# Attention and gated unit for one decoded token: the programs of ScalarE and VectorE aligned to a block of 256 instructions

## The chip, the cores and the metric

The kernel runs on one core of a Trainium2 chip. The metric is the device time of one execution, in microseconds, as the median of several runs; lower is better. The core has five engines with a program each: TensorE (PE), VectorE (DVE), ScalarE (ACT), GpSimd (POOL) and SyncE (SP), and 16 DMA engines that all of them share.

## The reference

One token `x` (512 values) is normalized and goes two ways: through attention with 32 heads over a cache of 8192 keys and values per head (128 wide), and through a gated unit of width 1376. The result is combined with `x`. All data are float32.

```python
x = A_x                                                        # 1 x 1 x 512
xn = _layernorm(x)
q = (xn @ A_wq).reshape(1, 1, 32, 128)                         # by heads
scores = einsum("bhqd,bhkd->bhqk", q, A_k_cache) * 128 ** -0.5 # 32 x 8192
o = einsum("bhqk,bhkd->bhqd", softmax(scores), A_v_cache)
s = o.reshape(1, 1, 4096) @ A_wo
h = sigmoid(xn @ B_w_gate) * (xn @ B_w_up)
g = silu(h @ B_w_down)
out = x + s * g
```

The two caches are 134 MB each, `A_wq` and `A_wo` 8.4 MB each.

## The kernel before, in words

The program is written out engine by engine, with semaphores set and waited for by hand inside one critical section; no scheduler moves anything. Helpers record each operation: `Steps` counts an engine's finished operations in its semaphore, `wait` makes an engine wait for such counts, and `load` (L131) issues a transfer.

The 32 heads are taken in 16 pairs. One pair's keys are one load of 8 MB into a buffer of 128 partitions by 64 KB, and so are its values. There are three such buffers: `slots[0]` and `slots[1]` take the keys of even and odd pairs, `slots[2]` takes `wq` at first, then the values of one pair after the other, and at the end the weights of the gated unit. SyncE issues all large loads on its queue: `wq`, the keys of pairs 0 and 1, then by turns values and keys, then the gated unit's weights, then `wo` in six pieces.

The start: ScalarE issues the load of `x_col` (2 KB) as its first work and `x_row` as its second (both through L131); VectorE fills constants (L168 to L176). When `x_col` is there, VectorE, TensorE and ScalarE normalize it (L180 to L198). TensorE multiplies with `wq` (L206), ScalarE copies the rows (L211), TensorE spreads each row over the partitions (L218), and ScalarE copies these into `q_all` (L225), two copies per 512 columns, which serve two pairs. Values of pair 0 are issued by SyncE (L161) when TensorE is done with `wq`.

The loop over pairs i:

- VectorE (`scores`): the product of keys and query in place (L281), its sum over each head's 128 columns (L282), and the maximum of the sums per partition (L284). It waits for the keys of pair i and the copies of the query. When L282 of pair i - 2 is done, SyncE may load the keys of pair i into the same buffer.
- TensorE (`pair`): turns the maxima (L246), spreads them (L248), sums the powers (L250), multiplies the powers with the values (L255), and picks the heads out of the result (L260). The first 15 pairs are a loop in TensorE's program, the last is written out.
- ScalarE (`powers_of`, `parts`, `place`): the scale of the maximum (L294), the exponentials (L296), the copy of the product with the values (L301), and the loads that put finished heads in their place in `o_all`.
- VectorE (`all_max`, `heads_out`): the maximum over a pair (L276), the quotient (L288, L289).
- When TensorE has done L255 of pair i, SyncE may load the next values.

Only TensorE's program has a loop; those of the other engines are written out in full. TensorE's loop is opened by this line, whose `head_slot` puts the loop's first instruction at the beginning of a block of 256 instructions:

```python
with nc.Fori(0, NP - 1, engines=OrderedEngineSet([PE.engine]), head_slot={PE.engine: 0}):
```

It does that with the directive that the change uses: an `addr_align` of 256 instructions, offset 0, `max_nops=0`. In the order of instructions it is an entry "ISA" on TensorE ahead of the loop's branch.

The end: TensorE computes the gated unit (L356 to L392, with VectorE and ScalarE), then the product with `wo` as its pieces land (L402, L406), and VectorE combines (L416, L418); SyncE issues the store.

The critical section is entered by all engines after SyncE's signal (L67); ahead of it ScalarE has one instruction that adds 16 to the semaphore `s_out`, which SyncE waits for at the end.

Of the kernel before, what the change touches and what calls it, by code (L numbers as in the profile page):

```python
# [18 lines left out]
def kernel(  # L19
# [40 lines left out]
    PE, DVE, ACT, SP, POOL = nc.tensor, nc.vector, nc.scalar, nc.sync, nc.gpsimd  # L60

    s_out = tc.alloc_semaphore("s_out")
    ACT.nop().then_inc(s_out, 16)
    section = ctx.enter_context(ExitStack())
# [391 lines left out]
```

## Time and profile before

| | before |
|---|---|
| median of 3 runs | 687.58 us |
| lowest and highest | 687.45 and 687.75 us |
| profiled execution: span from first to last instruction | 685.6 us |
| busy: VectorE | 574.0 us (84%) |
| busy: TensorE | 222.1 us (32%) |
| busy: ScalarE | 40.9 us (6%) |
| read from memory | 293.74 MB, 428 GB/s over the span |

The three runs were made without the profiler. Of the profiled execution the profile gives the span, not a time of its own beyond it; the 2.0 us between span and median lie around the first and last instruction.

How to read the rows that follow: a row of the order of time has the start and the length in us, the engine ("SPq" and "ACTq" are the issues of transfers by SyncE and ScalarE), the line, the operation, and in brackets the idle time before it and who ended it. A row of a DMA queue has the queue, the kind of its packets, their number, the megabytes, and the time that they took as a share of 16 engines. The kind "hardware_dynamic" is a kernel's transfers (q1 those that SyncE issues, q10 ScalarE's); the kind "instruction" is the loading of an engine's program. A row of a transfer's issue ends with the KB where they are given and the us from issue to landing. A row of stretches has the stretch, its length, the busy time of TensorE, its weight loads, VectorE, ScalarE and GpSimd, the clock granted to TensorE, the DMA share and the GB/s.

### The profile page before, as it was taken

The numbers are of one execution on the slowest core, as the hardware profiler recorded it, in microseconds if no ns is written. First come the engines' busy times: TensorE is split into PE (matmuls) and PEld (weight loads), VectorE is DVE, ScalarE is ACT, GpSimd is POOL, SyncE is SP. The second block draws the span as 40 slices with busy tenths as digits, with TensorE's granted clock in tenths as the row PEclk, the third lists the DMA queues.
The fourth block names the chain that finished last, engine by engine and source line by source line (L and its number), as shares of the span: only waits on it lengthen the run. The fifth ranks groups of instructions, "written<-read, shape, count | busy, mean of one in ns | idle before, by whom it ended". The sixth has DMA issues, their size and how long they took to land.

```text
span 685.6 us, 3694 instructions
## 1 busy us (share of the span) xinstructions
PE 222.1 (32%) x1570; PEld 62.7 (9%) x1570; DVE 574.0 (84%) x136; ACT 40.9 (6%) x122; POOL 0.7 (0%) x6
## 2 busy tenths in 40 slices
PE   0550230605041140505042140506042140605656
PEld 0110000101010010101001010101000010101121
DVE  0159999999999999989898989989898989989220
ACT  0040100000000000000001010000001010000010
POOL 0000000000000000000000000000000000000000
PEclk9965575757566575757557575756657575756798
DMA  9999999999999999999999999999999999999996
GB/s 375 440 445 451 428 428 428 432 428 428 428 436 444 448 440 428 428 428 436 428 428 428 440 444 451 428 432 428 432 432 428 428 440 436 451 436 428 405 434 285
DMA packets 6614, 293.84 MB, mean 429 GB/s; under 512 B 1096, under 2 KB 1104, under 8 KB 1616
## 3 DMA queue, kind: packets, MB, share of 16 engines
q1 hardware_dynamic: 6200, 293.74, 99.1%
q10 hardware_dynamic: 408, 0.02, 0.0%
q8 instruction: 4, 0.07, 0.0%
q14 instruction: 2, 0.02, 0.0%
HBM read 293.74 MB, written 0.00 MB: 428 GB/s over the span
## 4 chain that ended last, share of the span: by engine, by line
DMA 37%; DVE 30%; PE 0%; SPq 0%; issue 0%
DMA slot<-in_A_k_cache_dram 31%; DVE slot L281 15%; DVE sc L282 15%; DMA slot<-in_A_wo_dram 6%; PE acc L406 0%; SPq L131 0%; PE pt L246 0%; PE acc L377 0%; DVE g_row L416 0%; DVE g_row L418 0%; DVE mx L276 0%
## 5 line engine op out<-in xcount | busy, mean ns | idle before, releaser
L281 DVE TENSOR_TENSOR slot<-slot,q_all 128x16384 f32<-128x16384 f32 x16 | 275.5, 17217 | 38.8 <-DMA slot<-in_A_k_cache_dram 38.8
L282 DVE TENSOR_REDUCE sc<-slot 128x128 f32<-128x16384 f32 x16 | 275.5, 17220 | 0.6
L255 PE MATMUL po<-slot,weights 128*8 128x512 f32 x1024 | 146.7, 737 | 232.1 <-PEq L242 231.5
L255 PEld LDWEIGHTS po<-slot,weights 128*8 128x8 f32 x1024 | 30.3, 103 | 335.3 <-issue 334.6
L246 PE MATMUL pt<-ident,mx 128*1 128x128 f32 x32 | 8.8, 374 | 148.6 <-PEq L242 148.6
L301 ACT COPY o<-po 128x512 f32<-128x512 f32 x16 | 9.4, 586 | 385.2 <-PE po L255 385.2
L260 PE MATMUL pn<-o,pick 128*2 128x128 f32 x128 | 16.5, 272 | 12.8 <-PEq L242 12.8
L180 DVE TENSOR_REDUCE st<-x_col 128x1 f32<-128x4 f32 x1 | 0.2, 157 | 20.7 <-DMA x_col<-in_A_x_dram 20.7
L246 PEld LDWEIGHTS pt<-ident,mx 128*1 128x1 f32 x32 | 1.8, 80 | 154.1 <-issue 154.1
L288 DVE RECIPROCAL rl<-pn 2x1 f32<-2x1 f32 x16 | 2.3, 146 | 14.6 <-PE pn L260 14.6
L294 ACT ACTIVATE nb<-pm 128x2 f32<-128x2 f32 x16 | 2.8, 173 | 190.4 <-PE pm L248 190.4
L416 DVE TENSOR_TENSOR g_row<-g_row,acc 128x128 f32<-128x128 f32 x1 | 0.3, 289 | 15.3 <-PE acc L406 15.3
L296 ACT ACTIVATE weights<-sc,nb 64x128 f32<-64x128 f32 x32 | 12.8, 399 | 0.9
L260 PEld LDWEIGHTS pn<-o,pick 128*2 128x2 f32 x128 | 9.9, 84 | 29.6 <-issue 27.2
L248 PE MATMUL pm<-mx,ones 1*128 1x2 f32 x32 | 8.8, 344 | 7.4 <-PEq L242 7.4
L402 PE MATMUL big<-slot,o_all 128*1 128x512 f32 x56 | 9.4, 765 | 4.8 <-DMA slot<-in_A_wo_dram 4.8
L250 PE MATMUL pn<-rs,half 128*2 128x1 f32 x32 | 3.0, 163 | 23.5 <-PEq L242 23.5
L218 PE MATMUL big<-q_all,ones 1*128 1x512 f32 x16 | 8.8, 850 | 1.6 <-ACT q_all L225 0.8
L206 PE MATMUL big<-slot,xn 128*1 128x512 f32 x64 | 9.0, 726 | 0.8 <-DVE xn L198 0.8
L248 PEld LDWEIGHTS pm<-mx,ones 1*128 1x128 f32 x32 | 7.9, 306 | 14.4 <-issue 14.4
L276 DVE TENSOR_REDUCE mx<-pt 1x2 f32<-1x128 f32 x16 | 4.5, 278 | 5.2 <-PE pt L246 5.0
L182 PE MATMUL pt<-st,ones 128*128 128x1 f32 x2 | 0.6, 362 | 23.4 <-DVE st L180 23.4
(61 smaller groups left out, 62.1 us busy)
## 6 DMA issues: line engine op xcount, KB each, us to landing
slot<-in_A_wo_dram SPq DMA_DIRECT2D x1, 3584.0 KB, 32.5
slot<-in_B_w_gate_dram SPq DMA_DIRECT2D x1, 2752.0 KB, 16.8
slot<-in_B_w_up_dram SPq DMA_DIRECT2D x1, 2752.0 KB, 22.8
slot<-in_B_w_down_dram SPq DMA_DIRECT2D x1, 2560.0 KB, 27.3
slot<-in_A_wo_dram SPq DMA_DIRECT2D x1, 2560.0 KB, 38.2
slot<-in_A_wo_dram SPq DMA_DIRECT2D x1, 1024.0 KB, 40.2
o_all<-on ACTq DMA_DIRECT2D x32, 0.5 KB
slot<-in_A_wo_dram SPq DMA_DIRECT2D x1, 512.0 KB, 40.9
```

What stands on the lines that cost most here:

```text
L206: ins = PE.matmul(big[b][g * GP:g * GP + 1, :], xn[:, k:k + 1], wq_t[:, k, c:c + QT], start=(k == 0), stop=(k == KT - 1))
L218: spreads[t] = pe(PE.matmul(big[t % 2], ones[g * GP:g * GP + 1, :], q_row[g * GP:g * GP + 1, b, :], start=True, stop=True))
L246: PE.matmul(pt[0:1, :], mx[:, 0:1], ident, start=True, stop=True).then_inc(turned, 1)
L248: PE.matmul(pm, ones[:1, :], mx[:1, 1:3], start=True, stop=True).then_inc(spread_m, 1)
L255: ins = PE.matmul(po[g * GP:g * GP + 2 * HT, :], weights[:, j // HT, :], v[:, j * Dh:(j + HT) * Dh], start=(j < HT * NG), stop=(j >= NB - ...
L260: ins = PE.matmul(pn[:, :Dh], pick[:, b:2 * HT:HT], o1[:, b * Dh:(b + 1) * Dh], start=(b == 0), stop=(b == HT - 1))
L276: DVE.reduce_max(mx[:1, 1:3], pt[0:1, :].rearrange("o (e p) -> o e p", e=2), axis=AX.X).then_inc(reduced, 1)
L281: wait(DVE, dve(DVE.tensor_mul(k, k, qb[:, i:i + 1, :].to_broadcast([P, NB, Dh]))))
L282: summed[i] = dve(DVE.reduce_sum(sc[i % 2], k, axis=AX.X))
L296: ACT.activation(weights[h, :, e * HT:(e + 1) * HT], sc[i % 2][h].rearrange("p (g b) -> p g b", b=HT), AF.Exp, bias=nb[h, e:e + 1], scale= ...
L301: ACT.copy(o1, po).then_inc(copied, 1)
L402: ins = PE.matmul(big[0][g:g + 1, :], o_all[:, r:r + 1], wo_t[:, r, :], start=(r < NG), stop=(r + NG >= W_FOLD))
```

## The change

Two lines are put ahead of everything else in the programs of ScalarE and VectorE:

```diff
@@ -61,6 +61,8 @@
 
 
 
+    for eng in (ACT, DVE):
+        eng.addr_align(256, max_nops=0)
     s_out = tc.alloc_semaphore("s_out")
     ACT.nop().then_inc(s_out, 16)
     section = ctx.enter_context(ExitStack())
```

[...] `max_nops` is the number of padding instructions that the engine may execute; with 0 the first place of the padding is a branch to the aligned instruction. At most 255 places are put in. The two directives stand after the barrier with which each engine's program begins, and ahead of the critical section.

In the built program ScalarE and VectorE each have one more entry ("ISA", L65). On ScalarE it carries the addition to `s_out` as well. Nothing else is added, removed or moved; the lines of the kernel are numbered two higher.

## The prediction

> **What bounds the kernel now.** I read the page first (span, row of the DMA share, queues, chain), then the busy time by stretches, then the start in order of time, because the change touches only the start of two engines' programs.
>
> ```profile
> span 685.6 us, 3694 instructions
> ...
> DMA  9999999999999999999999999999999999999996
> ...
> q1 hardware_dynamic: 6200, 293.74, 99.1%
> ...
> q8 instruction: 4, 0.07, 0.0%
> q14 instruction: 2, 0.02, 0.0%
> ...
> DMA 37%; DVE 30%; PE 0%; SPq 0%; issue 0%
> ```
>
> The 16 DMA engines are at 90% or more in 39 of 40 slices, and SyncE's queue q1 alone fills 99.1% of them: the inputs are 293.74 MB and are read once. The last two queue rows are the loading of the engines' own programs, six packets in the whole span. The chain alternates between loads of K and the two long VectorE steps.
>
> ```profile
> 0.00:42.00 42.00, 15.30 (x80) 4.31 (x80) 4.24 (x22) 6.14 (x14) 0.70 (x6) 0.98 1.00 425
> 42.00:294.00 252.00, 73.23 (x477) 20.93 (x476) 246.92 (x40) 14.75 (x47) 0.00 (x0) 0.62 1.00 432
> 294.00:639.00 345.00, 102.52 (x700) 28.74 (x700) 318.42 (x53) 15.07 (x52) 0.00 (x0) 0.63 1.00 435
> 639.00:681.00 42.00, 29.85 (x292) 8.29 (x290) 3.89 (x19) 4.83 (x11) 0.00 (x0) 0.81 0.95 406
> ...
> L281 DVE TENSOR_TENSOR slot<-slot,q_all 128x16384 f32<-128x16384 f32 x16 | 275.5, 17217 | 38.8 <-DMA slot<-in_A_k_cache_dram 38.8
> ```
>
> The next to last column is the DMA share: 1.00 up to 639 us. VectorE (third busy column) is nearly full from 42 to 294 us (246.92 of 252), and from there it waits for K before each pair. In both stretches the transfers are continuous, so the end is the first packet's start, plus the bytes, plus a short tail after the last landing. A delay elsewhere costs time only if it leaves the DMA engines without a queued load.
>
> **The change part by part.** In the order of instructions on each engine, ScalarE and VectorE each gain one entry (the directive); every operation after it stands as before, and TensorE, GpSimd and SyncE are untouched. So the cost has three parts: a jump at the start with perhaps a wait for code, some extra packets of code, and another place at which later blocks of code come in.
>
> (a) *The jump at the start.* The kernel before has one such jump: TensorE's loop carries the same directive (offset 0, jump over the padding), as the order of instructions shows right ahead of the loop.
>
> ```profile
> 37.96 7.74 PE L218 MATMUL big<-q_all,ones 1*128 1x512 f32 x12 [0.84 <-ACT q_all L225]
> 77.23 0.58 PE L246 MATMUL pt<-ident,mx 128*1 128x128 f32 x2 [31.54 <-PEq L242]
> ```
>
> The DMA view of the stretch 48 to 50 us has one row of code loading (the first below); those of 193 to 194 and of 225 to 226 us have one each too, both with the same numbers (the second):
>
> ```profile
> q8 instruction: 1, 0.02, 3.0%
> ...
> q14 instruction: 1, 0.01, 1.9%
> ```
>
> TensorE's last matmul ahead of the loop ends at 37.96 + 7.74 = 45.70, and its first one in the loop is at 77.23, waiting for VectorE's maximum anyway. One packet of code is moved between 48 and 50 us, so I read q8 as TensorE's. From this row the jump is worth at most 50 - 45.7 = 4.3 us, and at least nothing (whether the packet holds the target or what follows it the trace doesn't tell). For ScalarE and VectorE I take 1 to 5 us. The DMA engines are empty at that moment, which favours the low end, but not for long:
>
> ```profile
> 0.96 0.39 SPq L131 DMA_DIRECT2D slot<-in_A_wq_dram  x1
> 0.97 0.41 ACTq L131 DMA_DIRECT2D x_col<-in_A_x_dram  x1
> 1.04 0.17 DVE L168 MEMSET ones<- 128x128 f32 x1 [1.04 <-SPq L67]
> ...
> q1 hardware_dynamic: 3, 0.20, 30.8%
> ...
> q1 hardware_dynamic: 16, 1.05, 102.5%
> ```
>
> The last two rows are the DMA view of 0 to 2 us and of 1.9 to 4.9 us: the first `wq` packets start just before 2 us, and until 4.9 us nothing but 16 of them moves, though ScalarE issued `x_col` at 0.97. A packet of code that comes after them waits as `x_col` did, to about 5 us.
>
> What is late then? VectorE's first fillings are needed by nothing for 20 us. ScalarE's first work is the issue of `x_col`, and from there goes a chain to the first product with K:
>
> ```profile
> slot<-in_A_wq_dram SPq DMA_DIRECT2D x1, 22.0
> x_col<-in_A_x_dram ACTq DMA_DIRECT2D x1, 2.0 KB, 22.1
> slot<-in_A_v_cache_dram SPq DMA_DIRECT2D x1, 46.6
> ...
> q1 hardware_dynamic: 129, 8.32, 98.8%
> q10 hardware_dynamic: 116, 0.00, 0.3%
> ...
> 23.14 0.16 DVE L180 TENSOR_REDUCE st<-x_col 128x1 f32<-128x4 f32 x1 [20.65 <-DMA x_col<-in_A_x_dram]
> 26.25 9.02 PE L206 MATMUL big<-slot,xn 128*1 128x512 f32 x64 [0.81 <-DVE xn L198]
> 37.15 1.54 ACT L225 COPY q_all<-big 64x256 f32<-64x256 f32 x4 [1.21 <-PE big L218]
> 42.28 17.23 DVE L281 TENSOR_TENSOR slot<-slot,q_all 128x16384 f32<-128x16384 f32 x1 [13.93 <-DMA slot<-in_A_k_cache_dram]
> ```
>
> The 2 KB of `x_col` take 22.1 us, as long as the 8 MB of `wq` issued with it. From 2 to 22 us (the q1 and q10 rows) the two queues move 129 and 116 packets, one tiny packet for each large one, and a large one takes 0.988 x 16 x 20 / 129 = 2.45 us. So `x_col` needs eight such rounds, and a later issue moves its landing by whole rounds. A wait of 1 to 5 us in ScalarE is worth 0 to 2 rounds, 0 to 4.9 us. I take one or two.
>
> *First cover.* The copies that pair 0 needs are the first two of the four at 37.15, done at about 37.9; VectorE starts at 42.28, released by K. That hides 42.28 - 37.9 = 4.4 us.
>
> *Second cover.* What goes beyond moves VectorE's first pair, and so the next load of K:
>
> ```profile
> 35.34 0.33 SPq L161 DMA_DIRECT2D slot<-in_A_v_cache_dram  x1
> 76.79 0.33 SPq L131 DMA_DIRECT2D slot<-in_A_k_cache_dram  x1
> ```
>
> V of pair 0 is issued at 35.34 and lands 46.6 us later, at 81.9; K of pair 2 is issued at 76.79. So q1 has 5.1 us of work left when that load comes, less about 1.0 us from issue to first packet (0.96 to 2 us, above): 4.1 us of cover. Both together hide 8.5 us, 3 rounds (7.35 us). With two rounds VectorE starts 0.5 us late, and the transfers do not notice. Contribution to the end: 0. If both covers were gone, each us of delay would cost one.
>
> (b) *Extra packets of code.* A q14 packet takes 1.9% of 16 x 1 us = 0.30 us of one DMA engine. Each engine may load the block that it jumps to and the one behind it: four more packets than before. On four different engines they hardly move the last landing; all on the one that ends last they cost 4 x 0.30 = 1.2 us. Below nothing: if the two packets at 193 and 225 us now fall where they don't count, 0.6 us is won. I take 0.2.
>
> (c) *Later blocks.* The two q14 rows fall into the middle of the run; here are the issues of K around them.
>
> ```profile
> 148.29 0.33 SPq L131 DMA_DIRECT2D slot<-in_A_k_cache_dram  x1
> 184.05 0.33 SPq L131 DMA_DIRECT2D slot<-in_A_k_cache_dram  x1
> 219.80 0.33 SPq L131 DMA_DIRECT2D slot<-in_A_k_cache_dram  x1
> 255.56 0.33 SPq L131 DMA_DIRECT2D slot<-in_A_k_cache_dram  x1
> ```
>
> The steps are 35.76, 35.75 and 35.76 us, with and without such a packet: these loads stop nobody, so there is no stall here for the alignment to remove. After the change they come in at a later pair, probably past 294 us, where VectorE waits 2 to 3 us per pair for K anyway (38.8 us in 10 waits, L281 above, 13.9 of them the first). Contribution 0.
>
> [...]
>
> *Sum.* 685.6 (profiled span) + 0 (a) + 0.2 (b) + 0 (c) = 685.8 us. The three runs shown have a median of 687.58, 2.0 us above the profiled span for what lies around it. Forecast: **687.8 us**, no change. A measurement of this kernel can tell about 0.2%, 1.4 us, from no change.
>
> **The rivals.**
>
> 1. *Slower: the wait for code outgrows the covers.* Place: ScalarE's jump ahead of `x_col`. If the packet of code waits behind two `wq` packets (to 7.4 us), and `x_col` then waits two rounds of its own, its first packet is at 12.3 instead of 4.9, 3 rounds, which is still covered; one more round, or a second block fetched in turn, makes it 4 or 5. It decides from 8.5 us on: 4 rounds cost 9.8 - 8.5 = 1.3 us, 5 cost 3.8. With the 0.2 of (b): 689.1 to 691.6 us. For it: `x_col` itself shows that nothing passes a 64 KB packet once it runs. Against it: the jump comes when the DMA engines are still idle, and TensorE's jump cost at most 4.3 us with them full. Here also lies the case that all packets of code hit the last DMA engine (+1.2).
> 2. *Nothing happens: the target is already loaded.* Both programs are short (136 and 122 counted instructions), and the padding could end in a block that has been loaded ahead. Then no wait, no `x_col` shift, and 687.6 us. Against it: TensorE's jump was followed by a packet.
> 3. *A little faster through fewer packets in the middle*: 0.6 us as in (b), 687.0 us. More can't be had: the shares of 1.00 leave no idle time in the transfers, and the tail ends on `wo` and TensorE, not on the two engines' code.
>
> **How the numbers follow.** Forecast (a wait inside the covers) 0.60; rival 1 0.15; rival 2 0.17; rival 3 0.05; 0.03 for a gain that I can't price. Within 0.2% lie the forecast, rivals 2 and 3: 0.82. Slower 0.15, faster 0.03. The predicted time is the forecast's, 687.8. The range goes from rival 3's 687.0 to 687.8 + 1.0 (the rest of (b)) + 0.5 (VectorE's late start, in case it isn't hidden) = 689.3; that leaves out most of rival 1 and the unpriced gain, under 0.2.
>
> **What would show it.** Right: q14 with about six packets, some in the first 10 us; `x_col` issued 1 to 5 us later, `L180` 0 to 5 us later, `L281`'s first start at 42.3 to 42.8; K of pair 2 issued before 77.5; the DMA row still all nines. Wrong in (a), if K of pair 2 is issued after 81 us and the DMA row has a lower digit there. Wrong in (c), if VectorE's or ScalarE's wait "issue" grows by microseconds in one pair. Wrong in (b), if the first packets and all steps stand as before and the last `wo` lands over 1 us later. Rival 2: ScalarE's first issue still at 0.97.

## The result, and the profile after

The changed kernel is slower: a median of 690.82 us (689.75 to 692.55, five runs) against 687.58 (687.41 to 687.75, five runs), a ratio of 1.0051 with a 95% interval of 1.004 to 1.0062. That is 3.2 us, and the runs also spread eight times as wide (2.8 us and 0.34). The time lies above the stated range (687.0 to 689.3), in rival 1.

The page of the changed kernel, the rows that answer to those shown of before:

```profile
span 688.0 us, 3696 instructions
...
DMA  9999999999999999999999999999999999999996
GB/s 375 454 446 428 373 427 427 457 453 427 431 427 427 427 427 438 465 434 431 427 427 427 427 427 427 427 457 453 431 427 428 427 427 427 446 457 427 402 434 284
...
q1 hardware_dynamic: 6200, 293.74, 98.9%
...
q8 instruction: 4, 0.07, 0.0%
q14 instruction: 6, 0.05, 0.0%
...
DMA 30%; DVE 25%; SPq 1%; PE 0%; issue 0%
```

The profiled run's span grew by 2.4 us; it was the fastest of the five (689.75). There are six packets of code on q14, four more than before. The row of the DMA share in tenths hides the loss, the row of GB/s doesn't: in the fifth slice (68.8 to 86 us) it falls to 373, where before it was 428. 55 GB/s over 17.2 us are 0.95 MB, or 2.2 us of transfer; that is a rough count, as a packet's bytes are put into the slice in which it starts. The row of before:

```profile
GB/s 375 440 445 451 428 428 428 432 428 428 428 436 444 448 440 428 428 428 436 428 428 428 440 444 451 428 432 428 432 432 428 428 440 436 451 436 428 405 434 285
```

The start in order of time, changed kernel (start, length, engine, line):

```profile
0.96 0.39 SPq L133 DMA_DIRECT2D slot<-in_A_wq_dram  x1
3.45 5.65 ACTq L133 DMA_DIRECT2D x_col<-in_A_x_dram  x1
3.84 0.17 DVE L170 MEMSET ones<- 128x128 f32 x1 [3.84 <-issue]
9.14 1.11 ACTq L133 DMA_DIRECT2D x_row<-in_A_x_dram  x1
30.72 0.16 DVE L182 TENSOR_REDUCE st<-x_col 128x1 f32<-128x4 f32 x1 [25.44 <-DMA x_col<-in_A_x_dram]
44.82 1.54 ACT L227 COPY q_all<-big 64x256 f32<-64x256 f32 x4 [1.21 <-PE big L220]
45.68 17.22 DVE L283 TENSOR_TENSOR slot<-slot,q_all 128x16384 f32<-128x16384 f32 x1 [9.75 <-ACT q_all L227]
80.18 0.33 SPq L133 DMA_DIRECT2D slot<-in_A_k_cache_dram  x1
```

SyncE starts as before, at 0.96. ScalarE reaches the issue of `x_col` 2.5 us later than before (0.97), and the issue itself takes 5.65 us in place of 0.41. `L182` comes 7.6 us later than its like before (23.14), and the first product with K, 3.4 us later (42.28), is no longer released by K but by ScalarE's copies of the query. K of pair 2 is issued 3.4 us later (76.79).

The DMA views of 1 to 2 us, of 7 to 8 us and of 529 to 533 us, changed kernel, have these rows of code loading:

```profile
q14 instruction: 2, 0.02, 4.2%
...
q14 instruction: 2, 0.02, 3.9%
...
q14 instruction: 2, 0.02, 1.0%
```

There are two packets ahead of the first `wq` packets (they start at 1.71 and 1.76 us), which I read as one for each engine; two more among the `wq` packets (7.50 and 7.59 us); and the last pair, which before came at 193 and 225 us. Each has 8192 bytes; the trace gives a packet's time and size, not what it holds. With one of the two engines aligned alone there are four packets on q14, two more than before. In the change's trace the first pair ends at 2.05 and 2.09 us, and ScalarE's first work follows at 3.45, 1.4 us behind it. The second pair ends at 7.8 and 7.9 us, and the long issue of `x_col` ends at 3.45 + 5.65 = 9.10, 1.2 us behind it.

### The profile page after: what moved, and what is told of

The parts are those of the page before. It is cut to its first block, busy times and chain, and to the rows that moved or that the text cites. A ratio compares the mean times of both kernels' runs of the same rounds, so it can differ in the third digit from the quotient of the medians.

```text
span 688.0 us, 3696 instructions
## 1 busy us (share of the span) xinstructions
PE 222.3 (32%) x1570; PEld 62.5 (9%) x1570; DVE 574.0 (83%) x136; ACT 40.9 (6%) x122; POOL 0.7 (0%) x6
## 4 chain that ended last, share of the span: by engine, by line
DMA 30%; DVE 25%; SPq 1%; PE 0%; issue 0%
DMA slot<-in_A_k_cache_dram 25%; DVE slot L283 13%; DVE sc L284 13%; DMA slot<-in_A_wo_dram 5%; SPq L133 1%; PE pt L248 0%; PE acc L408 0%; DVE g_row L418 0%; DVE g_row L420 0%; DVE mx L278 0%
## 5 line engine op out<-in xcount | busy, mean ns | idle before, releaser
L182 DVE TENSOR_REDUCE st<-x_col 128x1 f32<-128x4 f32 x1 | 0.2, 157 | 25.4 <-DMA x_col<-in_A_x_dram 25.4
L250 PEld LDWEIGHTS pm<-mx,ones 1*128 1x128 f32 x32 | 7.9, 305 | 14.5 <-issue 14.5
```

The lines of the kernel that those rows point to most:

```text
L250: PE.matmul(pm, ones[:1, :], mx[:1, 1:3], start=True, stop=True).then_inc(spread_m, 1)
```

## The experiments

The theories: **A**, ScalarE's jump makes `x_col` late, and so the query, the first pair and the load of K of pair 2, until the DMA engines run dry; **B**, VectorE's own late start counts; **C**, the additional packets of code on the DMA engines count. A1 to A3 in the expectations are three readings of the long issue: a wait for the second pair of packets ("the next block of code" there, which is my reading), the cost of any issue while the DMA engines are full, and the cost of any first issue after a jump. Each run below is the median of its own timed runs, beside the kernel before on the same chip.

| run | median, us (lowest to highest) | ratio to before (95% interval) |
|---|---|---|
| ScalarE aligned alone | 691.27 (690.81 to 692.07) | 1.0058 (1.0044 to 1.0071) |
| VectorE aligned alone | 688.21 (687.73 to 688.42) | 1.0008 (0.9999 to 1.0017) |
| both aligned to 128 | 687.45 (687.23 to 687.90) | 0.9999 (0.999 to 1.0008) |
| ScalarE's directive behind its issues | 688.12 (687.89 to 689.20) | 1.0012 (1.0003 to 1.0021) |
| `x_col` late by one filling, no alignment | 687.44 (687.28 to 687.87) | 1.0000 (0.9991 to 1.0009) |
| late by four fillings, no alignment | 690.71 (690.62 to 692.20) | 1.0050 (1.0036 to 1.0064) |
| late by six fillings, no alignment | 696.33 (695.99 to 696.40) | 1.0127 (1.0112 to 1.0143) |
| aligned, `x_col` issued by SyncE | 688.84 (688.24 to 690.06) | 1.0022 (1.0013 to 1.0031) |
| aligned, `x_col` late by three fillings | 691.95 (691.59 to 692.92) | 1.0068 (1.0054 to 1.0082) |
| both directives behind the first work | 689.33 (689.04 to 690.16) | 1.0024 (1.0014 to 1.0033) |

The kernel before was at 687.53 us in the first four and in the next four, and at 687.62 beside the last two. A trace is of one run each, and not always near the median: those of VectorE alone (688.42), of four fillings (692.20) and of both directives behind the first work (690.16) have the highest time of their row, and those of the change (689.75) and of the late aligned kernel (691.59) the lowest.

### One engine at a time

```diff
-    for eng in (ACT, DVE):
-        eng.addr_align(256, max_nops=0)
+    ACT.addr_align(256, max_nops=0)
```

> Only ScalarE's program is aligned to 256. Theory A (ScalarE's jump makes x_col late: the load is issued about 2.5 us late, its issue takes 5.7 instead of 0.4 us, x_col lands 7.6 us late, the query comes after K of pair 0, and the transfers run dry near 80 us): as slow as the change, 689.7 to 692.6 us, VectorE's L283 first at 45 to 48 us. Theory B (VectorE's own late start of 2.8 us is what counts): 687.6 us. Theory C (four more packets of code on the DMA engines): about half of the loss, 688.5 to 689.5 us.

```diff
-    for eng in (ACT, DVE):
-        eng.addr_align(256, max_nops=0)
+    DVE.addr_align(256, max_nops=0)
```

> Only VectorE's program is aligned to 256. Theory A: 687.4 to 687.9 us, x_col issued at 0.97 us and L283 first at 42.3 us, since nothing needs VectorE's first fillings for 20 us. Theory B: 689.7 to 692.6 us. Theory C: 688.5 to 689.5 us.

ScalarE alone gives the whole loss, 3.7 us. VectorE alone gives 0.7, with an interval that just touches no change; that hit none of the three ranges, as it is 0.3 us above A's and 0.3 below C's. B falls, and A carries the main part. The starts, in order of time, of ScalarE alone (first three rows) and of VectorE alone (last two):

```profile
3.67 5.59 ACTq L132 DMA_DIRECT2D x_col<-in_A_x_dram  x1
...
47.58 17.23 DVE L282 TENSOR_TENSOR slot<-slot,q_all 128x16384 f32<-128x16384 f32 x1 [10.10 <-ACT q_all L226]
...
82.08 0.33 SPq L132 DMA_DIRECT2D slot<-in_A_k_cache_dram  x1
```

```profile
0.97 0.41 ACTq L132 DMA_DIRECT2D x_col<-in_A_x_dram  x1
...
42.83 17.23 DVE L282 TENSOR_TENSOR slot<-slot,q_all 128x16384 f32<-128x16384 f32 x1 [13.94 <-DMA slot<-in_A_k_cache_dram]
```

With ScalarE alone the query is late, and VectorE waits for ScalarE. With VectorE alone `x_col` is issued as before, and VectorE's first pair is released by K, as before, but 0.55 us later than at 42.28, where A had expected no delay: the load of K itself lands later.

### How far the jump goes

```diff
-        eng.addr_align(256, max_nops=0)
+        eng.addr_align(128, max_nops=0)
```

> [...] If the loss of A comes from a target that is not loaded yet: 687.4 to 688.0 us, ScalarE issues x_col before 1.5 us. If any jump costs a load of code, or the next block is not held either: as slow as the change, 689.7 to 692.6 us, x_col issued near 3.5 us.

No loss: 687.45 us. ScalarE comes to the issue at 1.43 us, half a microsecond late, and ahead of any packet of code (the first starts at 1.91). So the target at the next multiple of 128 instructions was loaded here; with 256, ScalarE's first work came at 3.45 us, 1.4 us behind the end of the first packets. The issue still takes 2.55 us:

```profile
1.43 2.55 ACTq L133 DMA_DIRECT2D x_col<-in_A_x_dram  x1
...
42.72 17.23 DVE L283 TENSOR_TENSOR slot<-slot,q_all 128x16384 f32<-128x16384 f32 x1 [9.94 <-ACT q_all L227]
```

Here too packets of code come behind the jump: the trace has two, starting at 1.91 and 1.95 us and ending near 2.8, and the issue ends 1.2 us after. `L182` comes at 27.56 us, 4.4 us or nearly two rounds later than before, and VectorE now waits for the query, but starts only 0.4 us later than before; that is the first cover at its very end. The expectation that `x_col` is issued before 1.5 us held by its start alone.

### The same jumps where nobody waits

```diff
+    DVE.addr_align(256, max_nops=0)
...
     ld_x = load(ACT, "x", x_col, xv.rearrange("(p k) -> p k", k=KT))
...
     ld_xr = load(ACT, "xr", x_row[0:P:GP, :], xv.rearrange("(g c) -> g c", g=NG), c_xrow)
+    ACT.addr_align(256, max_nops=0)
```

> VectorE aligned at the start as in the change, ScalarE's directive moved behind its two issues of x_col and x_row. As many jumps and packets of code as the change. Theory A: 687.4 to 688.0 us, x_col issued at 0.97 us and landed at 22 us; ScalarE's wait for code lies in the 20 us in which it waits for x_col anyway. Theory C (packets of code) and any theory by which alignment itself is slow: 689.7 to 692.6 us.

688.12 us, just above the upper end of what A expected: both jumps and all packets of code of the change are there, and 2.7 of its 3.2 us are gone. What remains, 0.6 us, fits C, but is far less than the whole.

```diff
     ld_xr = load(ACT, "xr", x_row[0:P:GP, :], xv.rearrange("(g c) -> g c", g=NG), c_xrow)
+    ACT.addr_align(256, max_nops=0)
...
     c_big = [dve(DVE.memset(t, 0.0)) for t in big]
+    DVE.addr_align(256, max_nops=0)
```

> Both directives moved: ScalarE's behind its issues of x_col and x_row, VectorE's behind its first five fillings. Both jumps then lie in the 18 us in which both engines wait for x_col, and no engine is late for anything; what is left is packets of code on the DMA engines. If the 0.6 to 0.7 us of the two earlier runs (VectorE alone; ScalarE behind its issues) are packets: 687.9 to 688.5 us, K of pair 0 landing 0.3 to 0.9 us later on its last DMA engine. If they are VectorE's late start: 687.4 to 687.7 us.

A miss: 689.33 us, 1.7 above before, outside both ranges. No engine is late for anything that is needed here (the first two rows, and `L182` is still released by `x_col`), and yet in the profiled run (690.16) `x_col` and K of pair 0 land 1.7 us later than before:

```profile
0.97 0.41 ACTq L131 DMA_DIRECT2D x_col<-in_A_x_dram  x1
1.04 0.17 DVE L168 MEMSET ones<- 128x128 f32 x1 [1.04 <-SPq L67]
...
24.84 0.16 DVE L182 TENSOR_REDUCE st<-x_col 128x1 f32<-128x4 f32 x1 [22.36 <-DMA x_col<-in_A_x_dram]
...
43.98 17.23 DVE L283 TENSOR_TENSOR slot<-slot,q_all 128x16384 f32<-128x16384 f32 x1 [13.93 <-DMA slot<-in_A_k_cache_dram]
...
q14 instruction: 4, 0.03, 0.9%
```

The last row is the DMA view of 5 to 14 us: all four packets now fall among the `wq` packets, where in the change the first two came ahead of those (1.71 and 1.76 us). By themselves they take 0.9% of 16 x 9 us = 1.3 us, spread over the DMA engines. The times of the single packets show more. Which engine a packet is for isn't in the trace; but ScalarE's first work behind its jump, the load of a table, is at 9.27 us, 1.3 us behind the packet at 7.66, so I take that one and the one at 13.05 for ScalarE's and the other two for VectorE's. VectorE's two (0.31 us at 5.39, 0.32 at 11.08) stand in one gapless row with 64 KB packets, so probably on one DMA engine; the 64 KB packet behind the first takes 2.95 us, the one behind the second 3.08, and one with no packet of code ahead of it 2.42. That is 0.31 + 0.53 + 0.32 + 0.66 = 1.8 us on that DMA engine, the size of the delay of both landings (1.70). ScalarE's two (7.66 and 13.05) stand in another such row, with 1.2 us. So a packet of code cost 0.55 to 1.0 us here, its own time and what the packet behind it lost, and by this reading the two loads landed with the DMA engine that lost most. The change's trace has the same for its second pair: 0.31 us each, and 2.75 and 2.97 us for the 64 KB packets that start where they end. The span of this run grew by 2.8 us (688.4), so 1.1 of it is not in these two landings, and what the other nine runs lost isn't shown. That VectorE's 0.7 us are packets and not its late start fits this too: here it is on time, and with VectorE alone its second packet (at 7.63, the next 64 KB packet 2.95 us) came among `wq`.

### Late without a jump

In the next three runs nothing is aligned; ScalarE's issue of `x_col` waits for additional fillings of `q_all` by VectorE (N = 1, 4 and 6), which nothing else needs. Nothing of the result changes.

```diff
+    for _ in range(N):
+        c_late = dve(DVE.memset(q_all, 0.0))
+        wait(DVE, c_late)
+    ld_x = load(ACT, "x", x_col, xv.rearrange("(p k) -> p k", k=KT), c_late)
     c_ones = dve(DVE.memset(ones, 1.0))
```

> No alignment. ScalarE's issue of x_col waits for one extra filling of q_all by VectorE (about 1.9 us), so it comes near 3 us, as late as in the change, but with no code to load. Theory A1 (the 5.65 us that this issue takes in the change are a wait for the next block of code, whose packet ends at 7.8 us): the issue takes 0.4 to 0.6 us, x_col's first packet near 7.4 us, L281 first before 42.8 us, 687.3 to 687.9 us. Theory A2 (any issue by ScalarE takes over 5 us once wq's packets run): the issue ends near 9 us and the time is 689 to 691.5 us as in the change.

> No alignment. x_col waits for four such fillings, so its issue comes near 9 us, where it ends in the change. Theory A1: issue 0.4 to 0.6 us, x_col lands near 30 us as in the change, L281 first at 45 to 47.5 us, the transfers run dry by 0.5 to 3 us near 80 us, 689.2 to 692 us: the loss without any alignment. Theory A2: the issue ends near 14.7 us, 694 us or more. If a late x_col is not the cause: 687.5 us.

> No alignment. x_col waits for six fillings, its issue comes near 13 us, 4 us after that of the run with four. By the covers as the change showed them (4.4 us ahead of K of pair 0, then 2.5 us until the transfers run dry, then 1 us for 1 us, and about 0.7 us once for the restart): L281 first near 50.5 us, 692.5 to 695.5 us. If the loss were a fixed price for missing K of pair 0: as with four fillings, 689 to 692 us.

In order of time, the issue of `x_col` (ScalarE) and that of K of pair 2 (SyncE), with N = 1, 4 and 6:

```profile
3.24 0.40 ACTq L131 DMA_DIRECT2D x_col<-in_A_x_dram  x1
...
76.67 0.33 SPq L131 DMA_DIRECT2D slot<-in_A_k_cache_dram  x1
```

```profile
10.02 0.40 ACTq L131 DMA_DIRECT2D x_col<-in_A_x_dram  x1
...
82.70 0.33 SPq L131 DMA_DIRECT2D slot<-in_A_k_cache_dram  x1
```

```profile
14.53 0.40 ACTq L131 DMA_DIRECT2D x_col<-in_A_x_dram  x1
...
87.15 0.33 SPq L131 DMA_DIRECT2D slot<-in_A_k_cache_dram  x1
```

With N = 1 `x_col` is issued nearly as late (3.24) as after ScalarE's first wait in the change (3.45), and the time is 687.44: the first wait is covered. Its issue takes 0.40 us with the DMA engines full, so 5.65 us is not what an issue costs under load (A2 falls). With N = 4 the loss of the change is there without any alignment; the issue comes at 10.02, 0.9 us after it ends in the change, and VectorE's first product with K is at 48.19, later than the 45 to 47.5 that I expected. With N = 6 the median is above the expected range, because a filling with its wait took 2.26 us where I had put 1.9, and the issue came at 14.5 and not at 13. From four to six the load of K comes 4.45 us later and the profiled span grows from 690.3 to 694.3 us: about one for one, and no fixed price.

The traces of all late runs say the same, with and without a jump. The time of the profiled run less the moment at which K of pair 2 is issued is 689.75 - 80.18 = 609.6 us in the change, 691.27 - 82.08 = 609.2 with ScalarE alone, 692.20 - 82.70 = 609.5 with N = 4, 696.40 - 87.15 = 609.3 with N = 6, and 691.59 - 82.52 = 609.1 in the late aligned kernel below. So in these runs each us by which that load comes later than about 78 us (687.5 - 609.3) cost one.

### What the long issue waits for

```diff
+    for eng in (ACT, DVE):
+        eng.addr_align(256, max_nops=0)
...
-    ld_x = load(ACT, "x", x_col, xv.rearrange("(p k) -> p k", k=KT))
...
+    for _ in range(3):
+        c_late = dve(DVE.memset(q_all, 0.0))
+        wait(DVE, c_late)
+    ld_x = load(ACT, "x", x_col, xv.rearrange("(p k) -> p k", k=KT), c_late)
```

> Both programs aligned to 256 as in the change, and x_col waits for three fillings of q_all by VectorE, so that ScalarE comes to its issue near 10.6 us, after the next block of code is in (its packet ended at 7.8 to 9.1 us in four runs, the issue 1.2 to 1.4 us behind it). Theory A1 (the long issue is the wait for that block): the issue takes 0.4 us; the time is that of the run with four fillings and no alignment plus 0.3 to 1.0 us for packets of code, 690.6 to 693.5 us. Theory A3 (the first issue by ScalarE after a jump takes over 5 us whatever has been loaded): the issue ends near 16 us, x_col lands near 37 us or later, 696 us or more.

```profile
10.67 0.39 ACTq L133 DMA_DIRECT2D x_col<-in_A_x_dram  x1
```

The issue takes 0.39 us, the first one by ScalarE after its jump, once the second pair of packets is in (7.8 and 8.0 us), and the time of 691.95 us is in A1's range. A3 falls. In all four runs in which ScalarE, after its jump, came to an issue before that packet had ended, the issue ended 1.2 to 1.4 us after the last packet of that time: the change (packets end at 7.8 and 7.9, issue at 9.10), ScalarE alone (8.0 and 9.26), the alignment to 128 (2.8 and 3.98), and the next one (9.1 and 10.56, there it is `x_row`'s). VectorE's fillings in the change didn't wait so: they run from 3.84 us on, and the second pair of packets starts at 7.50 and 7.59.

### The query's load taken off ScalarE

```diff
+    ld_x = load(SP, "x", x_col, xv.rearrange("(p k) -> p k", k=KT))
     ld_wq = load(SP, "wq", wq_t, wq.rearrange("(p k) c -> p k c", k=KT))
...
-    ld_x = load(ACT, "x", x_col, xv.rearrange("(p k) -> p k", k=KT))
```

> Both programs aligned to 256 as in the change, but x_col is issued by SyncE ahead of wq, so that no issue of ScalarE lies on the way to the query. Theory A: L283 first before 43.5 us, what is left is the 0.6 us that VectorE's alignment alone cost, and up to 0.4 us for the issue ahead of wq: 687.8 to 688.8 us. If alignment costs in another way than through x_col: 689.7 to 692.6 us as in the change.

688.84 us, at the upper end of A's range (0.04 above it). 2.0 of the 3.2 us are gone although ScalarE is held as long as in the change (6.34 us, now in the issue of `x_row`, which nobody needs until the end).

```profile
4.22 6.34 ACTq L133 DMA_DIRECT2D x_row<-in_A_x_dram  x1
...
44.00 17.23 DVE L283 TENSOR_TENSOR slot<-slot,q_all 128x16384 f32<-128x16384 f32 x1 [29.16 <-DMA slot<-in_A_k_cache_dram]
```

VectorE is again released by K, which lands 1.7 us later than before: 0.45 of it because the issue of `x_col` stands ahead of `wq`'s and K's on SyncE; the rest fits the packets of code, as above. With 44.00 VectorE's start is later than the 43.5 expected under A; the 0.6 us taken there for packets don't explain it in full. No version came out below the kernel before, and none of the results points to one.

## Why the prediction was wrong, point by point

*What bounds the kernel* held, and also that a delay costs only if it leaves the DMA engines without a load. The change is a case of it, which these rows of busy time by stretches show, for before, the change, and N = 4 without alignment (the next to last column is the DMA time of packets that start in the stretch, the last their GB/s):

```profile
79.50:83.50 4.00, 1.60 (x10) 0.43 (x14) 4.00 (x1) 1.82 (x5) 0.00 (x0) 0.50 1.17 508
```

```profile
79.50:83.50 4.00, 1.14 (x4) 0.61 (x4) 3.20 (x4) 1.23 (x2) 0.00 (x0) 0.50 0.79 262
```

```profile
79.50:83.50 4.00, 0.36 (x2) 0.11 (x2) 3.46 (x2) 0.00 (x0) 0.00 (x0) 0.50 0.00 0
```

Before, packets of K of pair 2 follow those of V of pair 0 at once. In the change they start later, and only 16 of them; with N = 4 none starts in these 4 us.

*(a), the jump: the wait was of the size forecast, and another one behind it was missed.* The jump kept ScalarE from 0.97 to 3.45 us, inside the 1 to 5 us, and the run with N = 1 shows that this alone cost nothing. (The bound of 4.3 us from TensorE's jump took the engine to go on as soon as its packet is in; ScalarE's first work here came 1.4 us behind that.) The step that failed first is "I take one or two" rounds: it counts one wait. The trace has a second, in ScalarE's next transfer issue, which ended at 9.10 us, 1.2 us behind the second pair of packets of code. That pair came at 7.5 us, behind two `wq` packets. So the first packet of `x_col` moved from 4.9 to 12.1 us, three rounds. Rival 1, with its 0.15, named "a second block fetched in turn", and its range holds the result, but in part by luck: it counted on four or five rounds past covers of 8.5 us, and held three (with its first packet at 12.3) to be covered. What made three rounds cost time is the second cover.

*(a), the covers: the first was right, the second mis-sized.* The first cover's 4.4 us were there: the run aligned to 128, with `x_col` 4.4 us late, used them up and left VectorE 0.4 us late. The second I put at 4.1 us, from the landing of V of pair 0 at 81.9. That landing is the end on the last of 16 DMA engines. In the trace of before V's end marks stand between 79.9 and 80.6 us on fifteen engines and at 81.5 on one. From 76.79, with 0.96 us from issue to first packet (80.18 to 81.15 in the change), about 2.6 us were left. Three rounds minus 4.4, with what the copies add, made VectorE 3.4 us late, 0.8 too much.

*What running dry costs* was put at one for one. Measured over the DMA engines' idle time in the change's trace it is 0.9 us, and the first packets after it are longer: from the row above, 0.79 x 16 x 4.0 / 16 = 3.2 us each where a packet took 2.45. That adds 0.7. With 0.6 us for packets of code (taken from the runs with VectorE alone, and with ScalarE behind its issues; in the change itself it isn't told apart) this gives 2.2 of the 2.4 us by which the profiled span grew. By the late traces set side by side above, one for one holds from about 78 us on, so that the second cover was worth some 1.4 us (78.2 - 76.79) and not 4.1; the longer first packets are a part of what lies between that and 2.6, the rest isn't shown.

*(b), packets of code*: 0.2 forecast, 0.6 to 0.7 measured in the runs with ScalarE behind its issues and with VectorE alone, 1.7 in the worst. Two things failed: the price of one, 0.30 us, left out what the packet behind it loses (0.55 to 1.0 with it), and "on four different engines" is not how they seem to lie: in the trace of both directives behind the first work, two of them stand in one row of packets, and the other two in another. The upper bound of 1.2 us, all four on one, was passed for that reason with two on one.

*(c), later blocks* held: the packets came at 529.7 and 532.1 us, and the steps of K around them (issues at 485.35, 523.93 and 562.61) are 38.58 and 38.68 us, where those of before (483.57, 522.25 and 560.91) are 38.68 and 38.66.

The 0.17 for "already loaded" were answered by the run with 128: true there (`x_col` issued at 1.43 us, the first packet of code at 1.91), and not with 256 (ScalarE's first work at 3.45 us in place of 0.97, behind a packet of code).

*Left open.* The change's five runs reach from 689.75 to 692.55 us, and only the one of 689.75 was profiled. With ScalarE alone, issued 0.2 us later, `x_col` was done 1.6 us later (`L181` at 32.27), so a part of a round more or less is likely the spread; it wasn't shown for the other runs of the change. What the second pair of packets holds isn't shown. That ScalarE's issue waits for one of them, and not for something that ends with it, is read from the times alone (1.2 to 1.4 us between the two ends in four runs); why an issue would wait so isn't shown. That two packets of code shared a DMA engine is read from packet times that follow each other without a gap; why the packet behind one of them took longer isn't shown.

## What to carry to other kernels

An alignment by jump had its price here where it stood: 3.2 us with ScalarE's ahead of the issue of `x_col` (690.82). Keep the target inside code that is already loaded, which cost nothing here (687.45 us). Where the jump must go farther, put it behind the engine's first transfer issues, where it waits anyway; but packets of code then fell among the kernel's own loads, and the time was still 0.6 us longer (688.12) with ScalarE's directive moved and 1.7 (689.33) with both. For a chain that starts with a tiny load, count the time until its issue has ended, in rounds of the large packets among which it moves (2.45 us each here). And take a cover behind a load from the DMA engine that is done first (79.9 us here), not from the landing, which was the last one's (81.9).

## What the runs showed of the hardware that was not expected

- After a jump ScalarE's next transfer issue stayed until 1.2 to 1.4 us after the end of a packet of code that came behind the jump (the issues took 5.65, 5.59, 2.55 and 6.34 us in four runs), while it took 0.39 us in the run in which the second pair was in already.
- A packet of code of 8 KB among 64 KB packets took 0.31 us, and the 64 KB packet behind it 0.25 to 0.65 us more than 2.42 (2.66 and 2.95 us behind the two of before, 2.75 and 2.97 behind the second pair of the change, 2.95 and 3.08 with both directives behind the first work). In one trace, with two of them in one row of packets among the first loads, `x_col` and K landed 1.7 us later; the median of these runs is 1.7 us above before.
- In the change's trace the first 64 KB packets after the gap took 3.2 us and not 2.45.
